# Chunk 0 without the work on its zero state, and four zero fills on GpSimd

## The chip, the cores and the metric

The kernel runs on one core of a Trainium2 chip. The metric is the device time of one execution in microseconds. Three runs of the kernel before took 1280.0, 1281.79 and 1282.41 us, median 1281.79; the execution that the profiler recorded took 1282.63 us, and its trace spans 1280.9 us from the first to the last instruction.

## The reference

Three layers follow each other. The first is a recurrence over 768 steps for 4 x 8 heads with a 40 x 40 state that begins as zero:

```python
state = zeros(B, H, 40, 40)
for t in range(768):
    y[t]  = einsum('bhd,bhde->bhe', r[t], state)
    Sa    = einsum('bhde,bhe->bhd', state, a[t])
    state = state * w[t][:, :, None, :] - outer(Sa, b[t]) + outer(v[t], k[t])
```

Its output, 3072 rows of 320, goes through two gated layers: `(silu(x @ w_gate) * (x @ w_val)) @ w_out`, and the same with a sigmoid alone as the gate, both 320 to 1536 to 320. All of it is to hold in float32.

## The kernel before

The 768 steps are cut into 12 chunks of 64 (`NCH = 12`, `C = 64`). Inside a chunk the recurrence becomes matrix work: the inputs are scaled by running products of w, a triangular matrix is inverted, and the state passes from one chunk to the next through a few products. Four coroutines carry a chunk m:

- `prep_a(m)` turns the scaled inputs (`an`, `tkb`) on TensorE, copies them out on ScalarE, multiplies them (`kps`, L484), writes `bn` (ScalarE, L493 and L494) and the masked product `lq` (VectorE, L496). For chunks 0 to 3 the scaling comes from scans on VectorE (`first`, `scanned`), for the later ones from `powers`, which works mostly on GpSimd (L237), stores its results to DRAM (L267) and then loads the weights of the next four chunks into the same buffers (L235) and clamps them on VectorE (L240).
- `prep_b(m)` inverts the triangular matrix, `halves` for chunks 0 to 2 and `whole` for the others, mainly in small VectorE steps.
- `cp(m)` is `chain(m)` and then `post(m)`. `chain` copies the state `sT` into `qv` (ScalarE, L678), turns it with `tr4` (L680; the matmuls have the line of the helper, L369) and copies the turned state into `sd` (L681), multiplies (`qps` L688, `ups` L706, `sps` L719), and adds to the state (VectorE, L729 and L730). `post` forms the output: products with the new values (`aps`, L857) masked on VectorE, and then `yps` (L888) as a sum of two parts in one PSUM tile: part 0 is r times the state `sd`, part 1 the rest.
- `ahead(m)` runs a part of the first gated layer on the chunk before.

Beside them `early` and `more` load the gated layer's weights in pieces: a DMA (L996), an absolute value on ScalarE (L1004), a clamp on GpSimd (L1007), four VectorE steps (L1010 to L1016), a cast on ScalarE (L1026) and subtractions and sums on GpSimd (L1028 to L1034).

`first()` prepares chunk 0 in a PSUM region of its own. Its last readers are the copy of the scaling (L212) and that of `pend` (L177) on ScalarE; the banks of that region then serve everything else, `tr4` first.

The order of the program is written by `merge`, which takes steps of the coroutines by weights such as `QB` and `QN`. A planner then sets the order on each engine's queue from it and from a model of how long each instruction takes; each queue is worked in order on the chip, an instruction that waits holds up what stands behind it. The DMAs of the start are issued from one queue (SP).

`static` makes the buffers that stay. One with value 0.0 is put on the list `fills`, and `fill()` writes zeros to all on the list by ScalarE copies of a zero column (L81). It is called for `lq0` alone at L275 and for the rest at L944, in the program's order behind `prep_a(0)`. `ut`, `rbd` and the three `lq` have 2048 elements in each partition, the other buffers 256 to 1280. The values' and r's DMAs write into `ut` and `rbd` (L362, L363).

Of the kernel before, what the change touches and what calls it, by code (L numbers as in the profile page):

```python
# [18 lines left out]
P = 128  # L19
B, H, D = 4, 8, 40  # L20
W = 16
C = 64
# [4 lines left out]
PW = 64 + D  # L27
# [15 lines left out]
def attention(ctx, tc, st, ident, ins, banks, extra, early, more):  # L43
# [4 lines left out]
    nc = tc.nc  # L48
# [3 lines left out]
    dr = ctx.enter_context(tc.tile_pool(name="at_dram", bufs=2, space=DRAM))  # L52


    room, fills = {}, []

    def static(shape, name, val=None, part=None):
        sz = 1
        for x in shape[1:]:
            sz *= x  # L60
        if part is None:
            t = st.tile(shape, F32, tag=name, name=name)
        else:
            if part not in room:
                room[part] = [st.tile([P, 16 * P], F32, tag=part, name=part), 0]
            t, at = room[part]
            room[part][1] += sz
            t = t[:, at : at + sz]
            if len(shape) == 3:
                t = t.rearrange("p (x y) -> p x y", y=shape[2])  # L70
            if len(shape) == 4:
                t = t.rearrange("p (x y z) -> p x y z", y=shape[2], z=shape[3])
        if val == 0.0:
            fills.append(t)
        elif val is not None:
            nc.gpsimd.memset(t, val)
        return t
# [12 lines left out]
    E40 = (slice(0, 40), slice(64, 104))  # L90
# [127 lines left out]
    inv, done, out = {}, set(), {}  # L218
# [68 lines left out]
        )  # L287
    qv = static([P, 2, NS, D], "qv", 0.0, "part3")

    ut = static([P, 8, 4, 64], "ut", 0.0)  # L290
    rbd = static([P, 8, 2, 2, C], "rbd", 0.0)

    sT = static([P, 8, PW], "sT", 0.0, "part2")

# [26 lines left out]
    fills.append(x16)  # L321
    lq += [static([P, NS, 2, C], f"lq{i}") for i in (1, 2)]
    xinv = [static([P, NS, C], f"xinv{i}", part="part1") for i in range(2)]
    fills.extend(lq[1:])

    def loads(m):
        dma = nc.sync.dma_start
# [340 lines left out]
    def chain(m):  # L668
# [5 lines left out]
        def half(hb):  # L674
            pool, tag = ((pqu, "qu"), (pzy, "zy"))[hb]
            sg, s4 = slice(8 * hb, 8 * hb + 8), slice(4 * hb, 4 * hb + 4)
            for h2 in range(2):
                nc.scalar.copy(out=two(Q[E40[h2], h2, sg]), in_=pairs(sT, s4)[E40[h2]])  # L678

            ps = tr4(lambda n: sT[:, 4 * hb + n])  # L680
            nc.scalar.copy(  # L681
                out=sd[0:PW, s4], in_=ps[0:PW].rearrange("p n (h e) -> p n h e", h=2)[..., 0:D]
            )
            qps = pool.tile([P, 8, D], F32, tag=tag, name="qps")
            for n in range(8):
                q = 8 * hb + n
                for h2 in range(2):
                    nc.tensor.matmul(  # L688
                        qps[HALF[h2], n, :],
                        lhsT=L[:, q, h2, :],  # L690
                        rhs=Q[:, h2, q, :],
                        start=True,
                        stop=True,
                        tile_position=(0, 64 * h2),
                    )

            for h2 in range(2):
                nc.gpsimd.memset(L[HALF[1 - h2], sg, h2, :], 0.0)
            yield
            qs = wk.tile([P, 8, D], F32, tag="qs", name="qs", bufs=2)  # L700
            nc.scalar.copy(out=qs, in_=qps)
            ups = pool.tile([P, 8, D], F32, tag=tag, name="ups")
            for n in range(8):
                q = 8 * hb + n
                for h2 in range(2):
                    nc.tensor.matmul(  # L706
                        ups[HALF[h2], n, :], lhsT=X[HALF[h2], q, :], rhs=qs[HALF[h2], n, :], start=True, stop=True
                    )
            for h2 in range(2):
                nc.scalar.copy(out=Q[HALF[h2], h2, sg], in_=ups[HALF[h2]])  # L710
            last = nc.scalar.copy(out=pairs(us[hb]), in_=two(ups))
            if m == 1:
                marks["late"] = last
            yield
            sps = pool.tile([P, 8, D], F32, tag=tag, name="sps")
            for n in range(8):
                q = 8 * hb + n
                for h2 in range(2):
                    nc.tensor.matmul(  # L719
                        sps[E40[h2], n, :],  # L720
                        lhsT=T[:, q, 64 * h2 : 64 * h2 + D],
                        rhs=Q[:, h2, q, :],
                        start=True,
                        stop=True,
                        tile_position=(0, 64 * h2),
                    )
            sh = pairs(sT, s4)
            for e in E40:
                nc.vector.tensor_tensor(out=sh[e], in0=two(sps[e]), in1=sh[e], op=ALU.add)  # L729
            nc.vector.tensor_tensor(  # L730
                out=sh[0:PW],
                in0=sh[0:PW],
                in1=pend[0:PW, s4, :, None].to_broadcast([PW, 4, 2, D]),
                op=ALU.mult,
            )
            yield
# [104 lines left out]
    def post(m):  # L841
        pn = load_p(m)
        done.add(("q", m))
        T, sd = tkb[m % 3], sds[m % 2]
        ys = []
        for bp in range(2):
            ps = tr4(lambda n: us[bp][:, n])
            nc.scalar.copy(
                out=ut[0:PW, 4 * bp : 4 * bp + 4, 0:4:3], in_=ps[0:PW].rearrange("p n (h t) -> p n h t", h=2)
            )  # L850
            am, masked = [None, None], []
            for g2 in range(2):
                aps = pzy.tile([P, 2, 2, 2 * C], F32, tag="zy", name="aps")
                for n in range(2):
                    for h2 in range(2):
                        x = 4 * bp + 2 * g2 + n
                        nc.tensor.matmul(  # L857
                            aps[:, n, h2],
                            lhsT=ut[0:PW, x, 2 * h2 : 2 * h2 + 2].rearrange("p u s -> p (u s)"),
                            rhs=rbd[0:PW, x, h2].rearrange("p b t -> p (b t)"),  # L860
                            start=True,
                            stop=True,
                        )
                am[g2] = wk.tile([P, 2, 2, 2, C], F32, tag="am", name="am", bufs=2)
                masked.append(
                    nc.vector.tensor_tensor(  # L866
                        out=am[g2].rearrange("p n h b t -> p (n h b) t"),
                        in0=aps.rearrange("p n h (b t) -> p (n h b) t", b=2),
                        in1=mask[:, None, :].to_broadcast([P, 8, C]),
                        op=ALU.mult,  # L870
                    )
                )
                yield
            yps = pzy.tile([P, H, D], F32, tag="zy", name="yps")
            mats = []
            for part in range(2):
                for h in range(H):
                    hp, h2 = divmod(h, 2)
                    for b2 in range(2):
                        if part == 0:  # L880
                            x = 4 * bp + hp
                            lhs, rhs = rbd[0:PW, x, h2, b2], sd[0:PW, x, h2]
                        else:
                            q = 8 * bp + 2 * hp + b2
                            lhs, rhs = am[hp // 2][:, hp % 2, h2, b2], T[:, q, 64 * h2 : 64 * h2 + D]
                        with group(m, not mats):
                            mats.append(
                                nc.tensor.matmul(  # L888
                                    yps[HALF[b2], h, :],
                                    lhsT=lhs,  # L890
                                    rhs=rhs,
                                    start=part == 0 and h == 0,
                                    stop=part == 1 and h == H - 1,
                                    tile_position=(0, 64 * b2),
                                )
                            )
            if m >= FEW:
                tied(mats, masked)
            ysb = wk.tile([P, DM + 64], F32, tag="ysb", name="ysb", bufs=3)
            yf, pf = yps.rearrange("p h d -> p (h d)"), pn[:, DM * bp : DM * bp + DM]  # L900
            freed[:] = [
                nc.vector.tensor_tensor(out=ysb[:, x:y], in0=yf[:, z : z + y - x], in1=pf[:, z : z + y - x], op=ALU.mult)  # L902
                for x, y, z in ((0, DM, 0), (DM, DM + 64, 256))
            ]
            ys.append(ysb)
            yield
        out[m] = ys
# [32 lines left out]
    QW = (0.12, 0.2)  # L940
    QP = (0.02, 0.2)
    QN = (0.0714, -3)
    merge([(prep_a(0), 1, 0)])
    fill()  # L944
    for t, step in ((x16, 17), (xs, 34)):
        t = t.rearrange("p r t -> p (r t)")[:, ::step]
        nc.gpsimd.tensor_copy(out=t, in_=odd[:, 0:1].to_broadcast([P, 16]) if step == 34 else less.to_broadcast([P, 16]))
# [605 lines left out]
```

## Time and profile before

| | us |
|---|---|
| median of the runs | 1281.79 |
| profiled execution | 1282.63 |
| its span | 1280.9 |
| TensorE busy | 1195.3 |
| VectorE busy | 689.2 |
| ScalarE busy | 593.5 |
| GpSimd busy | 554.6 |

The busy times are sums over the whole span; they say which engine has most to do, not which one is waited for at a given time. For that the profile has a chain of waits, followed back from the last instruction, and a table that cuts the span into stretches. The recurrence ends near 640 us; from then on the gated layers run alone. PE is TensorE, PEld its weight load, DVE is VectorE, ACT ScalarE, POOL GpSimd, SP the engine that issues DMAs.

### The profile page before, as it was taken

What the parts mean: (1) busy time and instruction counts of PE and PEld (TensorE: products, weight loads), DVE (VectorE), ACT (ScalarE), POOL (GpSimd) and SP (SyncE); (2) the same over time, 40 slices, a digit from 0 to 9 for tenths busy, and PEclk for the clock granted to TensorE, in tenths of its full rate; (3) what the DMA queues carried; (4) which work ended last, traced back from release to release, by engine and by line L of the source; (5) the groups of instructions that cost most, each with busy time, mean ns of one, the idle gap of its engine ahead of it and who ended that gap; (6) DMA issues with size and microseconds to landing.
All of it is one profiled execution on the core that took longest, in us unless ns stands there. A gap on an engine that the chain in (4) does not pass through costs nothing.

```text
span 1280.9 us, 31386 instructions
## 1 busy us (share of the span) xinstructions
PE 1195.3 (93%) x12545; PEld 1080.0 (84%) x12545; DVE 689.2 (54%) x1432; ACT 593.5 (46%) x1447; POOL 554.6 (43%) x749
## 2 busy tenths in 40 slices
PE   5577989999999999899999999999999999999997
PEld 4467878889899889888898888889888888888886
DVE  6858559866886678875868544456221212121111
ACT  8454655656565655564443434345232323232222
POOL 5667243322332224356865766766322322232222
PEclk8667777999999999989999999999999999999999
DMA  8445544446544655254374543333010101000001
GB/s 220 129 119 144 166 112 126 109 103 156 128 104 115 136 131 118 65 127 129 88 269 128 181 139 135 103 115 91 1 46 1 46 1 34 1 21 1 21 1 25
DMA packets 180460, 124.38 MB, mean 97 GB/s; under 512 B 134608, under 2 KB 160208, under 8 KB 179536
## 3 DMA queue, kind: packets, MB, share of 16 engines
q1 hardware_dynamic: 180144, 122.11, 35.3%
q8 instruction: 101, 1.65, 0.5%
q14 instruction: 55, 0.45, 0.1%
q10 hardware_dynamic: 160, 0.16, 0.1%
HBM read 90.81 MB, written 31.43 MB: 95 GB/s over the span
## 4 chain that ended last, share of the span: by engine, by line
PE 61%; DVE 20%; ACT 8%; DMA 5%; issue 3%; POOL 2%; SPq 1%; DVEq 0%; ACTq 0%; POOLq 0%
PE g L1163 30%; PE po L1124 16%; PE gv L1108 5%; DVE pr L524 4%; DVE part L530 3%; PE kps L484 3%; DMA wt<-in_a_w_dram 2%; PE aps L857 2%; PE tp L369 1%; PE ups L783 1%; DVE lq L496 1%; DVE am L866 1%; ACT bn L494 1%; DVE g L1113 1%; ACT bn L493 1%
## 5 line engine op out<-in xcount | busy, mean ns | idle before, releaser
L1163 PE MATMUL g<-x,w 128*128 128x512 f32 (+1 forms) x1792 | 419.9, 385 | 0.8 <-DVE g L1170 0.7
L1163 PEld LDWEIGHTS g<-x,w 128*128 128x128 f32 x1792 | 323.2, 188 | 61.5 <-PE g L1163 1.1
L1172 POOL TENSOR_TENSOR hl<-g,hh 128x256 fp32r<-128x256 f32 x216 | 161.7, 754 | 282.4 <-ACT hh L1171 254.0
L1170 DVE TENSOR_TENSOR g<-g,g 128x256 f32<-128x256 f32 x216 | 82.1, 419 | 342.8 <-PE g L1163 340.4
L1124 PE MATMUL po<-w,hh 128*128 128x320 f32 x1152 | 233.7, 311 | 0.5 <-ACT hh L1114 0.4
L1124 PEld LDWEIGHTS po<-w,hh 128*128 128x128 f32 x1152 | 187.1, 188 | 9.6 <-ACT hh L1114 0.8
L1108 PE MATMUL gv<-x,w 128*128 128x256 f32 x1152 | 168.3, 293 | 4.8 <-DVE g L1113 2.5
L1171 ACT CAST hh<-g 128x256 fp32r<-128x256 f32 x216 | 86.9, 406 | 178.4 <-PE po L1124 168.3
L1108 PEld LDWEIGHTS gv<-x,w 128*128 128x128 f32 x1152 | 150.1, 195 | 7.7 <-DVE g L1113 3.4
L1124 PE MATMUL po<-w,hl 128*128 128x320 f32 x576 | 151.2, 313 | 3.7 <-POOL hl L1115 3.6
L1167 ACT ACTIVATE g<-g 128x256 f32<-128x256 f32 x216 | 72.9, 381 | 149.7 <-PE g L1163 143.2
L1115 POOL TENSOR_TENSOR hl<-g,hh 128x256 fp32r<-128x256 f32 x72 | 62.2, 864 | 138.8 <-ACT hh L1114 136.0
L1028 POOL TENSOR_TENSOR dt<-dt,w 128x384 f32<-128x384 f32 (+1 forms) x72 | 79.5, 1105 | 90.2 <-ACT w L1026 53.1
L1124 PEld LDWEIGHTS po<-w,hl 128*128 128x128 f32 x576 | 99.6, 188 | 5.4 <-POOL hl L1115 5.0
L496 DVE TENSOR_TENSOR lq<-kps,part 64x256 f32<-64x256 f32 x96 | 40.5, 422 | 78.6 <-ACT bn L494 72.4
L524 DVE TENSOR_TENSOR pr<-part,sn 128x4 f32<-128x4 f32 (+4 forms) x135 | 75.3, 558 | 3.7
L484 PE MATMUL kps<-lq,kbt 104*128 104x128 f32 x384 | 65.3, 323 | 11.5 <-DVE lq L496 8.6
L484 PEld LDWEIGHTS kps<-lq,kbt 104*128 104x128 f32 x384 | 57.0, 227 | 16.1 <-issue 4.5
L1010 DVE TENSOR_SCALAR dt<-dt 128x384 int32<-128x384 int32 (+1 forms) x72 | 40.5, 563 | 53.6 <-POOL dt L1007 53.3
L530 DVE TENSOR_REDUCE part<-pr 128x2 f32<-128x4 f32 (+4 forms) x135 | 66.6, 493 | 2.9
L857 PE MATMUL aps<-rbd,ut 104*128 104x128 f32 x384 | 56.9, 294 | 4.3 <-DVE ysb L902 1.7
L493 ACT ACTIVATE bn<-kps 32x256 f32<-32x256 f32 x96 | 35.8, 373 | 53.1 <-PE kps L484 40.8
(185 smaller groups left out, 1718.9 us busy)
## 6 DMA issues: line engine op xcount, KB each, us to landing
raw<-in_w_dram SPq DMA_DIRECT2D x48, 384.0 KB
xd<-x SPq DMA_DIRECT2D x12, 896.0 KB
x<-xd SPq DMA_DIRECT2D x11, 896.0 KB
raw<-in_w_dram SPq DMA_DIRECT2D x24, 320.0 KB
ld<-in_a_kb_dram SPq DMA_DIRECT2D x22, 320.0 KB
ld<-rd SPq DMA_DIRECT2D x64, 80.0 KB
pn<-pd SPq DMA_DIRECT2D x32, 160.0 KB
ld<-in_a_a_dram SPq DMA_DIRECT2D x12, 320.0 KB
```

The lines of the kernel that those rows point to most:

```text
L484: nc.tensor.matmul(kps[:, n].rearrange("p h t -> p (h t)"), lhsT=kbt[0:PW, n, :], rhs=lq[m % 3][0:PW, 4 * g4 + n].rearrange("p h t -> p (h ...
L524: nc.vector.tensor_tensor(out=o, in0=xs[:, 0:kk, None, 0:n].to_broadcast([P, kk, 2, n]), in1=sn[:, None, n : n + 2, 0:n].to_broadcast([P, ...
L530: nc.vector.tensor_reduce(out=xs[:, 0:kk, n : n + 2], in_=o, axis=AX.X, op=ALU.add)
L857: nc.tensor.matmul(aps[:, n, h2], lhsT=ut[0:PW, x, 2 * h2 : 2 * h2 + 2].rearrange("p u s -> p (u s)"), rhs=rbd[0:PW, x, h2].rearrange("p b ...
L1028: sub(out=tf, in0=tf, in1=w.bitcast(F32), op=ALU.subtract)
L1108: nc.tensor.matmul(gv[n], lhsT=p, rhs=q, start=e == 0, stop=e == len(seq) - 1)
L1124: self.nc.tensor.matmul(ops[u], lhsT=p[:, us], rhs=q, start=first and n == 0, stop=last and n == 2)
L1163: nc.tensor.matmul(gv[k][:, 0:n], lhsT=p, rhs=cols(at), start=e == 0, stop=e == len(seq) - 1)
L1167: nc.scalar.activation(out=g[j], in_=gv[0][:, j], func=AF.Silu if silu else AF.Sigmoid)
L1170: nc.vector.tensor_tensor(out=g[j], in0=gv[1][:, j], in1=g[j], op=ALU.mult)
L1171: nc.scalar.copy(out=hh, in_=g[j])
L1172: self.heng.tensor_tensor(out=hl, in0=g[j], in1=hh.bitcast(F32), op=ALU.subtract)
```

## The change

Three things are edited. In chunk 0 `half` no longer copies the state into `qv`, turns it and copies it into `sd`: the state is zero there, and `qv` holds zeros already. In `post` of chunk 0 only part 1 of `yps` is summed. And `ut`, `rbd`, `lq1` and `lq2` go on a list of their own, `sets`, which GpSimd fills by four memsets; both lists are filled ahead of `prep_a(0)` in the program's order.

```diff
-    room, fills = {}, []
-    def static(shape, name, val=None, part=None):
+    room, fills, sets = {}, [], []
+    def static(shape, name, val=None, part=None, fill=fills):
...
         if val == 0.0:
-            fills.append(t)
+            fill.append(t)
...
-    ut = static([P, 8, 4, 64], "ut", 0.0)
-    rbd = static([P, 8, 2, 2, C], "rbd", 0.0)
+    ut = static([P, 8, 4, 64], "ut", 0.0, fill=sets)
+    rbd = static([P, 8, 2, 2, C], "rbd", 0.0, fill=sets)
...
-    fills.extend(lq[1:])
+    sets.extend(lq[1:])
...
-            for h2 in range(2):
-                nc.scalar.copy(out=two(Q[E40[h2], h2, sg]), in_=pairs(sT, s4)[E40[h2]])
-            ps = tr4(lambda n: sT[:, 4 * hb + n])
-            nc.scalar.copy(
-                out=sd[0:PW, s4], in_=ps[0:PW].rearrange("p n (h e) -> p n h e", h=2)[..., 0:D]
-            )
+            if m:
+                (the same lines)
...
-            for part in range(2):
+            for part in (0, 1) if m else (1,):
...
-                                    start=part == 0 and h == 0,
+                                    start=part == (m == 0) and h == 0,
...
+    fill()
+    for t in sets:
+        nc.gpsimd.memset(t, 0.0)
     merge([(prep_a(0), 1, 0)])
-    fill()
```

## Rows read from the trace of the kernel before

**Rows 1.** The page's chain that ended last, shares of the span by engine.
```profile
PE 61%; DVE 20%; ACT 8%; DMA 5%; issue 3%; POOL 2%; SPq 1%; DVEq 0%; ACTq 0%; POOLq 0%
```

**Rows 2.** Stretches: us, busy us (x instructions) of PE, PEld, DVE, ACT, POOL, clock, DMA.
```profile
100.00:110.00 10.00, 6.04 (x85) 5.38 (x84) 10.00 (x18) 2.63 (x7) 6.74 (x9) 0.57 0.29 81
...
342.00:384.00 42.00, 40.83 (x679) 38.23 (x677) 31.82 (x65) 26.01 (x64) 12.96 (x15) 1.00 0.54 125
...
700.00:800.00 100.00, 100.00 (x523) 87.98 (x522) 52.67 (x113) 41.10 (x105) 67.41 (x91) 1.00 0.44 148
```

**Rows 3.** Order of time, ScalarE, 5 to 26 us: start, us, instruction [idle before <-releaser].
```profile
5.08 1.89 ACT L81 COPY ut<-part 128x2048 f32<-128x2048 f32 x1
...
6.88 1.89 ACT L81 COPY rbd<-part 128x2048 f32<-128x2048 f32 x1
8.68 3.52 ACT L81 COPY part<-part 128x832 f32<-128x832 f32 x6
...
12.41 3.69 ACT L81 COPY lq<-part 128x2048 f32<-128x2048 f32 x2
...
16.10 1.87 ACT L678 COPY part<-part 40x320 f32<-40x320 f32 x4
...
18.59 0.18 ACT L177 COPY pend<-f 104x16 f32<-104x16 f32 x1
...
24.98 0.51 ACT L1026 CAST w<-dt 128x384 fp32r<-128x384 f32 x1 [2.01 <-DVE dt L1011]
```

**Rows 4.** Order of time, TensorE, the product for `pend` and the first turns.
```profile
13.27 0.36 PE L175 MATMUL f<-part 128*104 128x16 f32 x2
...
18.82 1.95 PE L369 MATMUL tp<-ident,part 128*104 128x128 f32 x8 [5.20 <-ACT pend L177]
```

**Rows 5.** The chain of waits, 14 to 85 us: start, us, what.
```profile
14.83 1.50 DVE tkb L208 x2
...
16.49 1.69 DVE wp L240
...
18.25 2.17 POOL wp L237
...
79.36 5.62 DMA wq<-in_a_w_dram
```

**Rows 6.** Order of time, TensorE and VectorE, 78 to 104 us.
```profile
78.13 1.10 PE L369 MATMUL tp<-ident,part 128*104 128x128 f32 x4
...
83.59 1.45 PE L719 MATMUL sps<-part,tkb 128*40 128x40 f32 x46
...
85.18 1.49 DVE L240 TENSOR_SCALAR wp<-wq 128x2560 f32<-128x2560 f32 x1 [7.36 <-DMA wq<-in_a_w_dram]
...
91.06 0.99 DVE L729 TENSOR_TENSOR part<-sps,part 40x320 f32<-40x320 f32 x2
...
94.35 0.48 DVE L730 TENSOR_TENSOR part<-part,pend 104x320 f32<-104x320 f32 x1
...
101.63 1.94 PE L888 MATMUL yps<-part,rbd 104*64 104x40 f32 x32 [1.23 <-DVE am L866]
```

**Rows 7.** Groups by line, GpSimd: shapes xcount | busy us, mean ns | idle before.
```profile
L773 POOL MEMSET lq<- 64x1024 f32 x18 | 17.1, 953 | 20.1 <-PE qps L762 19.6
...
L698 POOL MEMSET lq<- 64x512 f32 x12 | 6.2, 519 | 0.6
```

**Rows 8.** Order of time, GpSimd, two waits before 40 us.
```profile
12.65 0.21 POOL L947 COPY x<-part 128x16 f32<-128x16 f32 x1 [8.96 <-ACT x L81]
...
38.66 1.01 POOL L1028 TENSOR_TENSOR dt<-dt,w 128x384 f32<-128x384 f32 x1 [2.93 <-DVE ds L1015]
```

**Rows 9.** Order of time, a clamp of 640 on VectorE, and GpSimd beside it.
```profile
10.18 0.50 DVE L155 TENSOR_SCALAR s<-s 128x640 f32<-128x640 f32 x1 [1.31 <-DMA s<-in_a_w_dram]
...
26.04 1.30 POOL L1028 TENSOR_TENSOR dt<-dt,w 128x384 f32<-128x384 f32 x1 [0.36 <-ACT bn L494]
...
26.40 1.29 DVE L155 TENSOR_SCALAR s<-s 128x640 f32<-128x640 f32 x1
```

More of the change, by code (lines that the diff above doesn't have):

```diff
@@ L676, in half @@
             sg, s4 = slice(8 * hb, 8 * hb + 8), slice(4 * hb, 4 * hb + 4)
-            for h2 in range(2):
-                nc.scalar.copy(out=two(Q[E40[h2], h2, sg]), in_=pairs(sT, s4)[E40[h2]])
-            ps = tr4(lambda n: sT[:, 4 * hb + n])
-            nc.scalar.copy(
-                out=sd[0:PW, s4], in_=ps[0:PW].rearrange("p n (h e) -> p n h e", h=2)[..., 0:D]
-            )
+            if m:
+                for h2 in range(2):
+                    nc.scalar.copy(out=two(Q[E40[h2], h2, sg]), in_=pairs(sT, s4)[E40[h2]])
+                ps = tr4(lambda n: sT[:, 4 * hb + n])
+                nc.scalar.copy(
+                    out=sd[0:PW, s4], in_=ps[0:PW].rearrange("p n (h e) -> p n h e", h=2)[..., 0:D]
+                )
             qps = pool.tile([P, 8, D], F32, tag=tag, name="qps")
```

## The prediction

> **What bounds the kernel now.** I read the page's chain by engine first, then the table of stretches, then the chain of waits from 0 to 150 us, and last the instructions of each engine in order of time where that chain passes chunk 0.
>
> The chain that ended last is TensorE's for 61% and VectorE's for 20%; ScalarE has 8% and GpSimd 2% [rows 1]. The reader is to see in the stretches where the rest sits: from 700 us on TensorE is busy 100 of 100 us, and in one chunk of the middle it is busy 40.83 of 42 us [rows 2]. Nothing of the change runs there. All that it touches lies before 105 us, where four engines wait for each other in turn. From 100 to 110 us VectorE is busy 10.00 of 10 us while TensorE has 6.04 [rows 2]. So the question is how much earlier VectorE leaves that stretch. A shift there should carry to the end nearly whole: what follows is bound by the order of work on TensorE and VectorE, and the weights that they then need are loaded when buffers come free, which moves with them.
>
> Two chains lead to that stretch, and they meet at 85 us.
>
> Chain A is chunk 0 itself. ScalarE fills buffers until 16.0 us (two of 2048 elements stand last, 12.41 to 16.0), makes four copies of the zero state (16.10 to 18.0), and only then copies `pend` at 18.59 [rows 3]. TensorE had that product ready at 13.63 (13.27 + 0.36), and its next work, the turns of `an`, sat idle for 5.20 us until `pend` was copied, because the first stage's PSUM banks are handed on only then [rows 4]. From there come the keys, the inverse, and at 78 to 85 us chunk 0's products.
>
> Chain B is the powers of w for chunks 4 to 7. VectorE's clamp (16.49) follows the keys, GpSimd's first product begins at 18.25, and after some 50 us of GpSimd work the results are stored and the next weights loaded into the same buffer (5.62 us from 79.36) [rows 5]. They land at 84.98. VectorE sat idle 7.36 us for them at 85.18, with all that stands behind the clamp in its queue, chunk 0's state sum at 91.06 among it [rows 6].
>
> **The change part by part.**
>
> *Fills.* Four of the 2048-element fills leave ScalarE: 1.89 for `ut`, the same for `rbd`, 3.69 for the two `lq` [rows 3], 7.47 us. On GpSimd the trace has 64x512 in 519 ns and 64x1024 in 953 ns [rows 7]; 434 ns for 512 more elements gives an estimate of 953 + 868 = 1.82 us for 2048, so 7.3 us for four. What hides them: GpSimd waited 8.96 us before its copy at 12.65 [rows 8], that is from 3.69 on. If that cover were gone, the powers at 18.25 would begin later by what overhangs, at most 7.3 us. The values' DMA into `ut` and `rbd` waits for these fills; `ut` was ready at 6.97 and would be by 3.69 + 1.82 = 5.5, and `rbd` at 7.3 instead of 8.8, so the DMA queue is not held longer.
>
> *Copies of the state on ScalarE.* Four at the start, 1.87 us together [rows 3], and one behind each group of turns, which the next item takes along.
>
> *What both do to chain A's beginning.* ScalarE would reach the end of the small fills at 5.08 + (12.41 - 8.68) = 8.8 us. `pend` is then bound by its product at 13.63, so about 13.7 instead of 18.59: 4.9 us. How much arrives is open. The keys that come next are multiplied on VectorE until 16.3 [rows 5], so the second step of chain A gains about that much too; but ScalarE's queue holds a cast of weights at 24.98 that waited 2.01 us for VectorE [rows 3], whose operand goes back over GpSimd to the clamp at 16.49, which does not move. Where that cast stays ahead of chunk 0's scalings, the gain ends there: 0. Where the planner puts the scalings ahead, all 4.9 arrives. It makes its order anew from a kernel whose ScalarE is free earlier, and no row tells which; I take half, 2.4, and keep 0 and 4.9 for the range.
>
> *Turns on TensorE.* Eight, in two groups of 1.10 us [rows 6] (one of the two stands there): 2.2 us out of a stretch in which TensorE runs one thing after the other and chunk 0's state product ends at 85.04 (83.59 + 1.45). It would end at 82.8, and with half of the first term at 80.4. VectorE is idle until 85.18 anyway. What decides is whether the state sums (0.99 for two at 91.06, as much for the next two, 0.48 for each of two scalings behind: 2.9 us) [rows 6] (the first of each pair stands there) run in that idle time or stay behind the clamp. In front: 2.9 us less in a stretch where VectorE is the bound. Behind: 0. I take half, 1.5, with 0 and 2.9 as ends.
>
> *Products of the state with r.* 32 matmuls, 1.94 us from 101.63 [rows 6]. VectorE is full there, so I put them at 0, with 1.9 as the other end.
>
> *Port shared by VectorE and GpSimd.* VectorE's clamp of 640 elements takes 0.50 us at 10.18 and took 1.29 us at 26.40, while GpSimd ran a subtraction from 26.04 to 27.34 [rows 9]: it waited about 0.8 us for GpSimd. The new fills may end only at 3.69 + 7.3 = 11.0, so the last can stand in the way of the clamp at 10.18, on chain B's way in. I take 0, with +0.8 as the bound by this row.
> The Trainium skill ("SBUF — State Buffer", section "Who interferes with whom") says that a VectorE instruction in a two-port mode, a `tensor_scalar` among them, and a GpSimd one exclude each other for a whole instruction. The row at 26.40 agrees; by the rule the wait could be a whole fill, 1.82 us, and the sum 1 us worse than by the row. No row here has a zero fill beside such a clamp.
>
> *Sum.* 2.4 + 1.5 = 3.9 us less. The profiled execution took 1282.63 us, 1.73 more than its span; less 3.9 that is 1278.7. It lies 0.84 above the median of the runs, 1281.79, so I forecast 1277.9, rounded to 1278. Ends: 4.9 + 2.9 + 1.9 = 9.7 less (1272.1), and 0.8 more (1282.6) without a change of order to the bad.
>
> **The rivals.**
>
> *Chain B decides alone* (no change). Nothing removed lies on it; the cast keeps its place on ScalarE and the state sums theirs behind the clamp. For it speaks that the next weights landed within 0.1 us of the state product's end, so whatever chain A saves is slack at once. Against it, that GpSimd itself waited 2.93 us at 38.66 for VectorE [rows 8], and so takes part in chain A's delays. Time: 1281.8, with 1.5 us to either side.
>
> *Everything arrives.* The planner puts chunk 0 ahead on both queues, and GpSimd's wait at 38.66 shrinks too. 4.9 + 2.9 = 7.8 less: 1274.0. Against it: three orders must all fall well.
>
> *GpSimd is held longer* (slower). Chunk 0's earlier inverse puts its small VectorE steps ahead of the weights' steps on VectorE, and GpSimd, which works in order, stands at its weight subtraction with the powers behind it. The place is the wait at 38.66, now 2.93 us [rows 8]. Each microsecond more there moves the store, the load and the clamp at 85.18 by as much. One more such wait is +2.9, two are +5.9; the middle gives 1281.8 + 4.4 = 1286.2. It decides from the point where the added wait is longer than what the state sums save (0 to 2.9). For it: chain B has no slack. Against: less work has to be done before 85 us on every engine but GpSimd, which idled.
>
> *A fill in front of the clamp.* The fill that runs at 10.18 holds VectorE's clamp for its whole length by the rows of smaller ones, 1.82 us [rows 7, 9]; chain B is as late, and chain A's gain stays unused: 1283.6. The Trainium skill's page named above has this as its rule.
>
> **How the numbers follow.** Forecast (2.6 to 6.5 us less, its own range 1275.3 to 1279.2): 0.38. Everything arrives: 0.14. Chain B alone: 0.24. Port: 0.06. GpSimd held: 0.18. A measurement of this kernel tells about 0.2%, 2.6 us, from no change. Faster: 0.38 + 0.14 = 0.52. Within: 0.24 + 0.06 = 0.30. Slower: 0.18. For 8 in 10 the range goes from 1271, one beyond the far end of the gains, to 1287, one beyond the middle of the slow case: a new order on the queues can add or take a little anywhere.
>
> **What would show it.** Right: `pend` copied by 14 us; TensorE's idle time before the turns of `an` gone; no fill of 2048 elements on ScalarE but the first; GpSimd's four at 1.8 us before 11 us; the state sums of chunk 0 before the clamp of the second group; VectorE through its full stretch 3 to 5 us earlier, and the same distance at the first wide matmul of the next stage near 699 us. Wrong: the cast of weights still ahead of the first scaling with the same time at both; the second load into the powers' buffer no earlier than 79.4 and all VectorE work behind it; or a later GpSimd chain, with its waits on VectorE grown. If the distance is there at 110 us and gone at 700, the claim that a shift carries is wrong.

## The result, and the profile after

Four runs of the changed kernel took 1291.32 to 1297.23 us, median 1293.58; four of the kernel before 1280.0 to 1282.41, median 1281.24. The ratio is 1.0102, with a 95% interval from 1.0076 to 1.0128. The change costs 12.3 us; 1278 had been forecast. The profiled execution took 1297.23 us, its span is 1295.5.

The page's chain by engine hardly differs from [rows 1]:

```profile
PE 62%; DVE 19%; ACT 8%; issue 4%; DMA 4%; POOL 3%; SPq 0%; ACTq 0%; POOLq 0%; DVEq 0%
```

The stretches of [rows 2], with the same columns, show that TensorE is as busy in the middle as before (40.74 of 42 us) and nearly so from 700 us on (98.18 of 100). Most of the loss lies between them:

```profile
100.00:110.00 10.00, 7.75 (x55) 7.36 (x52) 9.14 (x23) 3.65 (x8) 7.34 (x8) 0.66 0.61 200
342.00:384.00 42.00, 40.74 (x672) 38.07 (x673) 31.20 (x64) 25.48 (x62) 12.59 (x16) 1.00 0.55 123
700.00:800.00 100.00, 98.18 (x506) 85.21 (x505) 56.18 (x122) 39.61 (x101) 65.17 (x89) 1.00 0.43 140
```

The start of the changed kernel in order of time, engine by engine. A line of the kernel before has 1 more here from L680 on, and 3 more from L947 on (L1113 is now L1116):

```profile
2.38 1.81 POOL L946 MEMSET ut<- 128x2048 f32 x1
4.12 1.81 POOL L946 MEMSET rbd<- 128x2048 f32 x1
5.86 3.55 POOL L946 MEMSET lq<- 128x2048 f32 x2
...
4.64 5.19 DVE L155 TENSOR_SCALAR sn<-sn 128x640 f32<-128x640 f32 x1 [1.54 <-DMA sn<-in_a_w_dram]
...
11.54 2.40 PE L162 MATMUL f<-ident,bn 128*64 128x64 f32 x40 [11.54 <-DVE bn L147]
...
17.95 0.17 ACT L177 COPY pend<-f 104x16 f32<-104x16 f32 x1 [2.42 <-PE f L175]
...
19.88 1.53 PE L369 MATMUL tp<-ident,part 128*104 128x128 f32 x8 [1.97 <-DVE part L169]
```

The fills take 1.8 us each, as estimated. But VectorE's first clamp, for which all of chunk 0 waits, begins at 4.64 and lasts 5.19 us, to 9.83: it ends when the last fill (5.86 + 3.55 = 9.41) is over, and 0.42 us of its own. [Rows 9] have the same clamp of 640 elements at 0.50. So `pend` is copied at 17.95, only 0.64 us earlier than in [rows 3], and the turns of `an` begin 1.06 us later than in [rows 4].

At 82 us chunk 0's state sums (L730 here) have moved ahead of the clamp of the second group, as the prediction wanted; in [rows 6] they stood behind it at 91.06:

```profile
81.85 0.99 DVE L730 TENSOR_TENSOR part<-sps,part 40x320 f32<-40x320 f32 x2 [0.15 <-PE sps L720]
...
86.92 1.49 DVE L240 TENSOR_SCALAR wp<-wq 128x2560 f32<-128x2560 f32 x1 [1.71 <-DMA raw<-in_w_dram]
```

In these two traces the last step of a chunk's inverse (L617 for the first chunks, L534 for the later ones) comes 3.3 us earlier than before at 131 us, 7.1 earlier at 222, 1.7 at 256, at the same time at 301 and 0.8 later at 509. Then the next chunks' `ups` come 4.8 us late (559.1 for 554.3) and 7.5 late (603.2 for 595.7); a `g` of the next layer (L1170 before) is 13.8 us late at 691, and the spans end 14.6 apart. The gain is given back near 260 us, and the loss begins near 540 and grows in steps until about 700.

Only the first of these steps is followed here. VectorE's `g` is the product that a gated layer takes on; ScalarE casts it to `hh` for TensorE, and GpSimd makes `hl` of what the cast leaves over. `am` (L866) is the masked product of `post`; `pr` (L524) and the sum behind it (L530) are steps of the inverse. Before, in order of time:

```profile
538.53 0.41 DVE L1113 TENSOR_TENSOR g<-gv,g 128x256 f32<-128x256 f32 x1
538.87 0.56 DVE L524 TENSOR_TENSOR pr<-part,sn 128x400 f32<-128x400 f32 x1
...
539.44 0.86 PE L1124 MATMUL po<-w,hh 128*128 128x320 f32 x4
...
540.72 1.12 PE L857 MATMUL aps<-rbd,ut 104*128 104x128 f32 x8
542.63 1.13 PE L888 MATMUL yps<-part,rbd 104*64 104x40 f32 x32 [0.79 <-DVE am L866]
543.58 1.11 PE L888 MATMUL yps<-tkb,am 128*64 128x40 f32 x32
...
546.27 0.90 PE L1054 MATMUL xtp<-ident,ysb 128*128 128x128 f32 x3 [1.58 <-DVE ysb L902]
```

and after:

```profile
539.20 0.35 DVE L1018 TENSOR_SCALAR ds<-dt 128x384 int32<-128x384 int32 x1
539.87 0.55 DVE L1019 SCALAR_TENSOR_TENSOR ds<-raw,ds 128x384 f32<-128x384 uint32 x1
540.33 0.57 DVE L524 TENSOR_TENSOR pr<-part,sn 128x400 f32<-128x400 f32 x1
540.93 0.57 DVE L530 TENSOR_REDUCE part<-pr 128x20 f32<-128x400 f32 x1
541.42 0.41 DVE L1116 TENSOR_TENSOR g<-gv,g 128x256 f32<-128x256 f32 x1
...
542.33 1.28 PE L1127 MATMUL po<-w,hh 128*128 128x320 f32 x4 [2.73 <-ACT hh L1117]
...
544.54 2.07 PE L858 MATMUL aps<-rbd,ut 104*128 104x128 f32 x8 [0.41 <-DVE am L867]
547.40 1.94 PE L889 MATMUL yps<-part,rbd 104*64 104x40 f32 x32 [0.78 <-DVE am L867]
549.13 1.91 PE L889 MATMUL yps<-tkb,am 128*64 128x40 f32 x32
...
551.71 0.90 PE L1057 MATMUL xtp<-ident,ysb 128*128 128x128 f32 x3 [0.67 <-DVE ysb L903]
```

`g` is 2.9 us later, and TensorE stands 2.73 us for it. VectorE's queue now has four weight steps ahead of it (L1013 to L1019, two of them shown) and one pair of inverse steps more than before, the two of 400 elements at 540.33 and 540.93. The products that follow take 2.07 for 1.12 us and 1.94 for 1.13. The stretches tell why; the third number from the end is the granted clock. Before:

```profile
540.00:543.00 3.00, 2.19 (x24) 1.67 (x25) 2.96 (x6) 0.43 (x1) 0.27 (x1) 1.00 0.16 55
543.00:551.00 8.00, 6.42 (x127) 5.90 (x123) 7.77 (x12) 3.50 (x9) 3.47 (x5) 0.64 0.70 172
```

After:

```profile
540.00:543.00 3.00, 0.67 (x3) 0.67 (x4) 2.93 (x6) 0.41 (x1) 0.58 (x1) 0.92 0.45 129
543.00:551.00 8.00, 6.81 (x77) 6.00 (x75) 7.22 (x10) 0.85 (x2) 0.16 (x1) 0.50 0.24 75
```

Behind the wait TensorE has the lower of its two clocks all through; before, it had it for a part of that stretch. VectorE is busy 2.96 and 2.93 us of the first 3, so whatever its queue puts ahead of `g` or `am` there makes them later.

### The profile page after: what moved, and what is told of

It is laid out like the page before. It is cut to its first block, busy times and chain, and to the rows that moved or that the text cites. A ratio compares the mean times of both kernels' runs of the same rounds, so it can differ in the third digit from the quotient of the medians.

```text
span 1295.5 us, 31265 instructions
## 1 busy us (share of the span) xinstructions
PE 1197.2 (92%) x12473; PEld 1081.2 (83%) x12473; DVE 688.7 (53%) x1432; ACT 584.2 (45%) x1437; POOL 563.9 (44%) x753
## 4 chain that ended last, share of the span: by engine, by line
PE 62%; DVE 19%; ACT 8%; issue 4%; DMA 4%; POOL 3%; SPq 0%; ACTq 0%; POOLq 0%; DVEq 0%
PE g L1166 30%; PE po L1127 16%; PE gv L1111 4%; DVE pr L524 3%; PE kps L484 3%; DVE part L530 2%; PE aps L858 2%; PE tp L369 2%; DMA wt<-in_a_w_dram 2%; ACT bn L493 1%; ACT bn L494 1%; DVE am L867 1%; DVE dt L1014 1%; PE ups L784 1%; DVE lq L496 1%
## 5 line engine op out<-in xcount | busy, mean ns | idle before, releaser
L1127 PE MATMUL po<-w,hh 128*128 128x320 f32 x1152 | 237.4, 313 | 5.8 <-ACT hh L1117 5.4
L1111 PE MATMUL gv<-x,w 128*128 128x256 f32 x1152 | 171.0, 298 | 8.6 <-DVE g L1116 5.4
L1111 PEld LDWEIGHTS gv<-x,w 128*128 128x128 f32 x1152 | 153.4, 200 | 12.4 <-DVE g L1116 7.6
L1127 PE MATMUL po<-w,hl 128*128 128x320 f32 x576 | 154.5, 315 | 6.3 <-POOL hl L1118 5.6
L1170 ACT ACTIVATE g<-g 128x256 f32<-128x256 f32 x216 | 73.0, 382 | 153.9 <-PE g L1166 145.2
L524 DVE TENSOR_TENSOR pr<-part,sn 128x4 f32<-128x4 f32 (+4 forms) x135 | 74.3, 551 | 3.7
L484 PE MATMUL kps<-lq,kbt 104*128 104x128 f32 x384 | 62.1, 312 | 8.7 <-DVE lq L496 6.6
L530 DVE TENSOR_REDUCE part<-pr 128x2 f32<-128x4 f32 (+4 forms) x135 | 66.6, 493 | 2.9
L858 PEld LDWEIGHTS aps<-rbd,ut 104*128 104x128 f32 x384 | 52.2, 210 | 12.4 <-DVE am L867 8.7
L1007 ACT ACTIVATE dt<-raw 128x384 f32<-128x384 f32 (+1 forms) x72 | 38.4, 534 | 53.3 <-POOL w L1035 38.2
```

What stands on the lines that cost most here:

```text
L484: nc.tensor.matmul(kps[:, n].rearrange("p h t -> p (h t)"), lhsT=kbt[0:PW, n, :], rhs=lq[m % 3][0:PW, 4 * g4 + n].rearrange("p h t -> p (h ...
L524: nc.vector.tensor_tensor(out=o, in0=xs[:, 0:kk, None, 0:n].to_broadcast([P, kk, 2, n]), in1=sn[:, None, n : n + 2, 0:n].to_broadcast([P, ...
L530: nc.vector.tensor_reduce(out=xs[:, 0:kk, n : n + 2], in_=o, axis=AX.X, op=ALU.add)
L858: nc.tensor.matmul(aps[:, n, h2], lhsT=ut[0:PW, x, 2 * h2 : 2 * h2 + 2].rearrange("p u s -> p (u s)"), rhs=rbd[0:PW, x, h2].rearrange("p b ...
L1111: nc.tensor.matmul(gv[n], lhsT=p, rhs=q, start=e == 0, stop=e == len(seq) - 1)
L1127: self.nc.tensor.matmul(ops[u], lhsT=p[:, us], rhs=q, start=first and n == 0, stop=last and n == 2)
```

## The experiments

Two theories. *Order*: the change makes the planner set other queues, and these, not the changed work, cost the late 13 us. *Pace*: the changed work itself shifts the arrival of weights against the recurrence, and the late loss follows from that in any order. Each run was timed in five rounds beside the kernel before, whose medians then were 1279.8 to 1281.7 us; a time stands with its ratio to the kernel before and the 95% interval. Single executions of one kernel lie up to 12 us apart (e13), so verdicts go by the ratios, and distances between two traces serve only to find places.

**Each half alone.** e1 has the fills and the old chunk 0, e2 the new chunk 0 and the old fills; against the changed kernel:

```diff
# e1
-            if m:
+            if True:
...
-            for part in (0, 1) if m else (1,):
+            for part in (0, 1):
...
-                                    start=part == (m == 0) and h == 0,
+                                    start=part == 0 and h == 0,
# e2
-    ut = static([P, 8, 4, 64], "ut", 0.0, fill=sets)
+    ut = static([P, 8, 4, 64], "ut", 0.0, fill=fills)
... (rbd and the two lq in the same way)
+    merge([(prep_a(0), 1, 0)])
     fill()
-    for t in sets:
-        nc.gpsimd.memset(t, 0.0)
-    merge([(prep_a(0), 1, 0)])
```

> The four fills on GpSimd, both lists filled early; chunk 0 keeps the work on its zero state. Order theory (the 13 us come from another order on the queues in the last part of the recurrence, which only both halves of the change together bring about): this kernel's queues are those of the kernel before from about a quarter of the program on, so 1281 +- 4 us. Port theory (the fills hold VectorE's first clamp for 5 us, and that costs the time): 1286 or more.

> Chunk 0 without the work on its zero state; all fills stay on ScalarE where they were. Order theory: queues as before from a fifth of the program on, less work ahead of it, 1277 to 1282 us. Pace theory (the earlier chunk 0 itself, whatever the order, meets a lower clock or other transfers later): 1290 or more.

e1: 1277.80, ratio 0.9978 (0.9962 to 0.9993). e2: 1273.39, 0.9927 (0.9898 to 0.9955). Both halves gain, e2 more than either of its theories had, and e1 although its first clamp too lasts 5.13 us; together they lose 12.3: no sum of local costs does that. In their traces VectorE, ScalarE and GpSimd have the order of before from the first quarter on, but for a few entries; only with both halves do neighbours change again, between some 40 and 80% of the queue (VectorE's to 90%), for up to two thirds of the entries in a tenth of ScalarE's and GpSimd's.

**The late order, taken away and put in.** From here on some kernels have a written order. `QUEUES` lists each engine's instructions in the order of another kernel, and each gets a dependency on the one ahead of it that adds no wait:

```diff
+def pin(tc):
...
+    known = {i.name: i for i in tc.nc.cur_bb.bb.instructions}
+    for names in json.loads(zlib.decompress(base64.b85decode(QUEUES))).values():
+        names = [x for x in names if f"I-{x}" in known]
+        for x, y in zip(names[1:], names):
+            tc.add_manual_dep(known[f"I-{x}"], f"I-{y}", mybir.DependencyInfo(
+                mybir.DependencyClass.NoSync, mybir.DependencyReason.DATA), reason="order on the engine")
...
+    pin(tc)
```

e3 is the changed kernel with the order of before on the last 70% of each queue; e4 is the kernel before with the changed kernel's order there.

> The whole change, with its own order in the first 30% of each engine's instructions and the order of the kernel before forced on the rest. Order theory: the 3 us that the changed kernel was ahead at 255 us stay or are lost, the 13 us are gone: 1277 to 1283 us. Pace theory: 1290 to 1297 us as the changed kernel.

> The kernel before, all its work, with the changed kernel's order forced on the last 70% of each engine's instructions. Order theory: 1290 to 1297 us without any of the change. Pace theory: 1281 us.

e3: 1279.66, 0.9994 (0.9977 to 1.0011). e4: 1293.38, 1.0083 (1.0056 to 1.0109). The loss goes with the order, with the work on either side. The stretches 510 to 600 and 600 to 705 us, before, e3 and e4 in turn:

```profile
510.00:600.00 90.00, 83.07 (x1355) 78.21 (x1352) 60.62 (x127) 47.88 (x114) 45.23 (x64) 0.96 0.41 116
600.00:705.00 105.00, 99.29 (x844) 92.92 (x843) 81.84 (x168) 45.33 (x111) 71.61 (x94) 1.00 0.49 155
```
```profile
510.00:600.00 90.00, 83.41 (x1384) 78.55 (x1384) 60.40 (x127) 47.99 (x115) 45.70 (x64) 0.96 0.43 118
600.00:705.00 105.00, 99.59 (x847) 93.26 (x847) 81.15 (x168) 45.75 (x111) 71.94 (x94) 1.00 0.48 155
```
```profile
510.00:600.00 90.00, 80.88 (x1234) 75.91 (x1235) 58.40 (x122) 44.74 (x105) 42.27 (x56) 0.91 0.39 104
600.00:705.00 105.00, 96.87 (x869) 92.48 (x868) 76.42 (x150) 43.71 (x109) 69.30 (x94) 0.93 0.47 152
```

In the first e4 does 1234 matmuls where the others do 1355 and 1384, at a granted clock of 0.91 for 0.96. The pace theory falls.

**What the parts are worth with the order held.** All queues in the order of before, with chunk 0 alone (e5), the fills alone (e6) and both (e7); the edit is `pin(tc)`.

> Chunk 0 without the products, turns and copies of its zero state, fills as before, and every engine's queue in the order of the kernel before: what the removed work is worth by itself, with no re-planning. The prediction's own sum, with no port and the fills still on ScalarE, was the turns, copies and state sums (-1.5 us) and the products r x state (0 to -1.9 us), carried whole: 1278 to 1280. Queue-order theory: the 7 to 8 us that this half won with its own queues are partly the order's, so here the gain is smaller, 1277 to 1280. Rival (the removed work itself is worth it, order or not): 1273 to 1274, as with its own queues.

> The four fills on GpSimd, chunk 0 as before, every queue in the order of the kernel before. The first clamp on VectorE should again take 5.2 us and the first turns start 4.4 us later. Theory (local effect of the fills is a late start of chunk 0, paid back only in part by the freed ScalarE): 0 to 4 us slower, 1281 to 1285, and the lead of 5 us that the fills alone had with their own queues was the order's. Rival (the freed ScalarE stretch is worth more than the late clamp costs): 1277 to 1279 as with its own queues.

> The whole change with every queue in the order of the kernel before, so that neither the first nor the last part is re-planned. Queue-order theory: no late loss (as with the late order alone put back), and the lead that the change has up to 255 us is no longer lost near 260 us, since there too it was the new order: 1275 to 1279. Rival (the lead near 260 us is lost to a transfer whose time does not depend on the order): 1279 to 1282, no better than with the late order alone put back.

e5: 1279.08, 0.9992 (0.9981 to 1.0004). e6: 1284.16, 1.0035 (1.0022 to 1.0047). e7: 1284.69, 1.0034 (1.0023 to 1.0046). The removed work is worth 0.8 us, no more than the noise; the fills cost 4.3 us alone, and 5.6 on top of the removed work. e7's expectation of 1275 to 1279 failed, and so did its rival: in the order of before the change has no lead that could be lost near 260 us; so the lead that the changed kernel had was its early order's.

**The clamp.** e10 is e7 with the first two fills behind VectorE's first clamp and the other two behind its second:

```diff
...
-        nc.vector.tensor_scalar(out=xw, in0=xw, scalar1=WLOW, scalar2=WHIGH, op0=ALU.max, op1=ALU.min)
+        clamps.append(nc.vector.tensor_scalar(out=xw, in0=xw, scalar1=WLOW, scalar2=WHIGH, op0=ALU.max, op1=ALU.min))
...
-    for t in sets:
-        nc.gpsimd.memset(t, 0.0)
+    held = [nc.gpsimd.memset(t, 0.0) for t in sets]
...
     merge(start)
+    for k, x in enumerate(held):
+        tc.add_manual_dep(x.ins, clamps[k // 2].ins.name, mybir.DependencyInfo(
+            mybir.DependencyClass.Sync, mybir.DependencyReason.DATA), reason="behind a clamp")
```

> The whole change in the queue order of before, with one thing moved: the first two fills on GpSimd wait for VectorE's first clamp, the other two for its second clamp, so that neither stands behind fills. With the fills in front the same kernel was 4.9 us slower than before. Port theory (the held clamp is nearly all of it): the clamp takes 0.5 us again, the first turns start near 7.1 us, and the time is 1278 to 1281. Rival (fills on GpSimd hurt elsewhere, by later holds of VectorE or by what stands behind them in GpSimd's queue): 1283 to 1286, as with the fills in front.

1278.55, 0.9990 (0.9974 to 1.0007): 6.1 us less than e7, as the port theory has it. Its start in order of time:

```profile
4.54 0.49 DVE L155 TENSOR_SCALAR sn<-sn 128x640 f32<-128x640 f32 x1 [1.45 <-DMA sn<-in_a_w_dram]
...
5.16 1.81 POOL L945 MEMSET ut<- 128x2048 f32 x1 [1.47 <-DVE sn L155]
...
9.67 3.55 POOL L945 MEMSET lq<- 128x2048 f32 x2 [0.49 <-DVE s L155]
...
13.22 0.17 ACT L177 COPY pend<-f 104x16 f32<-104x16 f32 x1 [2.15 <-PE f L175]
...
15.42 1.72 PE L369 MATMUL tp<-ident,part 128*104 128x128 f32 x8 [2.23 <-DVE part L169]
```

The clamp is back at 0.49, `pend` is copied by 14 us, as the prediction had it, and the turns begin 3.4 us earlier than in [rows 4]. Yet the end is only 1.2 us earlier, which the interval does not tell from nothing. These four kernels have one order; where their chains stand, in us against the kernel before:

| | turns of `an` (chain A) | GpSimd's first power (chain B) | second group's clamp | end (medians) |
|---|---|---|---|---|
| e5 | -1.92 | -0.42 | -0.17 | -0.8 |
| e6 | +1.06 | +3.40 | +3.13 | +4.3 |
| e7 | +1.05 | +3.39 | +3.39 | +4.8 |
| e10 | -3.40 | -1.07 | -1.74 | -1.2 |

The clamp of the third column is the row at 85.18 in [rows 6]. In e7 and in e10 it waits as long as there for the load that ends chain B:

```profile
88.57 1.49 DVE L240 TENSOR_SCALAR wp<-wq 128x2560 f32<-128x2560 f32 x1 [7.53 <-DMA wq<-in_a_w_dram]
```
```profile
83.44 1.49 DVE L240 TENSOR_SCALAR wp<-wq 128x2560 f32<-128x2560 f32 x1 [7.40 <-DMA wq<-in_a_w_dram]
```

So at 85 us the held clamp costs through chain B: the clamp of the powers at 16.40 comes later on VectorE, at 19.80 in e7, and GpSimd's 50 us of powers move with it. That the end follows chain B is not shown. The sizes of its columns fit the medians better than chain A's, but e10 frees both chains at once, and the first three columns are of single executions: in e6's own trace the 3.13 us have shrunk to 0.79 at 301 us (L534), and in e10's the 1.74 have grown to 6.24. The -0.42 of e5 is scatter: e4 and e8, which start with all the work of before, have the first power at 17.82 and 17.54, for 18.25 in [rows 5].

**The early order by itself.** e9 is the work of before in the queues of e2; e11 is e10's work in them. The edit is again `pin(tc)`.

> All the work of the kernel before, with every queue in the order that the kernel with chunk 0 alone had (it ran 7 us faster; with the queues of before the same work was worth 0.8 us). If the order made those 7 us, they are here too, less about 1 us: 1273 to 1276. If it takes the removed work and the order together (the room that the left-out products and copies give is what the order fills): 1278 to 1282.

> The change with its fills behind the clamps and every queue in the order of the kernel with chunk 0 alone: the fastest order seen with the port kept free. If what the parts showed adds up, the freed ScalarE and no late loss: 1270 to 1274, at or below the 1273.4 of chunk 0 alone. If the fills still cost 3 to 4 us there: 1276 to 1278.

e9: 1279.80, 0.9998 (0.9982 to 1.0014). e11: 1275.58, 0.9958 (0.9941 to 0.9975). So e2's 7 us need both: the order alone gives 0.0, the left-out work alone 0.8. e11 lies between its two ranges; taking the fills off ScalarE adds nothing to e2, which stays the fastest kernel, ahead of the one before and of the changed one.

**Which queue holds the late loss.** e8 has the changed kernel's late order on TensorE alone, e12 on the other four alone; the work is that of before.

> The work of the kernel before; TensorE's queue alone has the order of the changed kernel over its last 70%, all the others keep the order of before. It tells which queue holds the 12 us that all five cost together. If TensorE's own order is at fault: 1288 to 1294. If it is the order on VectorE, ScalarE and GpSimd (the step that makes the expert part's input stands behind weight steps and inverse steps there, and TensorE only waits for it): 1280 to 1284.

> The work of before; VectorE, ScalarE, GpSimd and SyncE have the order of the changed kernel over their last 70%, TensorE keeps that of before. TensorE's order alone cost 10 us, all of it at one place near 647 us, while the five together lost theirs in steps from 540 to 650 us. If the steps are the other four's: 1288 to 1294, with +6 us by 560 us. If TensorE's order carries the loss however the others stand: 1280 to 1284.

e8: 1289.80, 1.0070 (1.0056 to 1.0085). e12: 1294.76, 1.0116 (1.0095 to 1.0138). The other four queues are enough for the whole loss, in steps from 540 us on (0.8 us over the first of its ranges). TensorE's order alone costs too, and e8's time fits the first of its two expectations, but not the reason: nothing is lost up to 640 us, and then, near the end of the recurrence, TensorE has the next layer's products ahead in its queue and stands for their load:

```profile
648.57 3.76 PE L1163 MATMUL g<-x,w 128*128 128x256 f32 x16 [5.25 <-DMA x<-xd]
```

The two don't add up (10.0 and 15.0, all five 12.9 in e4): each of these kernels mixes two orders, so neither says what share of the loss its queues have in the changed kernel.

**Which entry.** e13 puts four of VectorE's weight steps, 1.6 us, behind the `g` of 541.42, e15 puts them behind that chunk's last inverse step; e14 is the control, the changed kernel with its own order written out.

```diff
# VectorE's queue in e13
-... pr dt ysb ysb part0 dt pr ds part0 ds pr part0 g pr part0 ...
+... pr ysb ysb part0 pr part0 pr part0 g dt dt ds ds pr part0 ...
# and in e15
+... pr ysb ysb part0 pr part0 pr part0 g pr part0 ... x1t dt dt ds ds x x ...
```

> The changed kernel in its own order, but for four of VectorE's 1433 instructions: the four weight steps that stand ahead of the expert part's `g` at 541.4 us stand behind it. Together they take 1.6 us there. In the changed kernel TensorE stood 2.7 us for that `g`, and its next 136 or so matmuls ran at half the clock, 2.6 us longer than before. If that is how the first +5 us of the late loss comes about, the wait falls to about 1.2 us, and the clock either stays (4 us back at 551 us) or still falls (1.6 us back); carried to the end 1289.5 to 1292. Rival (the weights of the next expert, now 1.6 us later, are what is late, and the place is only where it shows): 1293 to 1295, nothing back by 560 us.

> The changed kernel with its own order written out by the same means with which the other orders were put into these kernels. If writing an order out costs nothing by itself: 1292 to 1295, like the changed kernel. If it does, it differs by more than 2 us, and all runs with a written order would have to be read against this one.

> As the pinned changed kernel, but the same four weight steps stand behind the last step of that chunk's inverse (`x1t`), past TensorE's whole wait, not just behind the `g`. Put behind the `g` they only moved the wait: TensorE then stood 2.6 us for `am` instead of 2.6 us for `hh`. If what costs is any 1.7 to 2 us of weight steps on VectorE between the two, because VectorE has no idle time there and TensorE falls to half its clock when it waits, then here TensorE's wait falls below 1 us, the clock stays at full speed through 543 to 551 us, and the next chunk's `ups` starts 3 to 5 us earlier than in the pinned changed kernel; at the end 1291 to 1294 (the later steps of the loss stay). Rival (the weights, 8 us later now, are late themselves and hold ScalarE's queue): no gain by 560 us, 1296 to 1300.

e14: 1296.86, 1.0112 (1.0087 to 1.0137), 1.9 us over its range, but with the ratio of the change itself (1.0102): writing an order out costs nothing that shows. e13: 1297.09, 1.0113 (1.0081 to 1.0144): nothing back, and 2.1 us over even the rival's range. The wait for `hh` went from 2.64 us (e14) to 1.80, and the one for `am` rose from 0.76 to 2.57. TensorE of e13 in order of time:

```profile
540.84 1.33 PE L1127 MATMUL po<-w,hh 128*128 128x320 f32 x4 [1.80 <-ACT hh L1117]
...
545.32 2.07 PE L858 MATMUL aps<-rbd,ut 104*128 104x128 f32 x8 [2.57 <-DVE am L867]
```

e15: 1301.54, 1.0161 (1.0147 to 1.0175), slower still and over both of its ranges. Both waits were short there (1.81 and 0.76), but the clock fell all the same:

```profile
543.00:551.00 8.00, 6.54 (x101) 5.77 (x100) 7.36 (x11) 0.00 (x0) 0.00 (x0) 0.50 0.00 0
```

The 0.00 on ScalarE and GpSimd is the new loss. The DMA queue holds a load into the weights' buffer, and that buffer is free only when the late weight steps have read it: the load is issued at 552.24 (539.40 in e14), with the transfers for `ob`, the layer's output, behind it. ScalarE stands for these, and TensorE's next inputs stand behind that copy in its queue. DMA queue, ScalarE and TensorE of e15:

```profile
552.24 0.33 SPq L999 DMA_DIRECT2D raw<-in_w_dram  x1
552.65 0.38 SPq L1767 DMA_DIRECT2D xs<-ob  x1
...
556.31 0.42 ACT L1766 COPY ob<-po 128x320 f32<-128x320 f32 x1 [15.42 <-DMA xs<-ob]
...
557.69 2.24 PE L1111 MATMUL gv<-x,w 128*128 128x256 f32 x7 [4.66 <-ACT x L1063]
```

Neither try gave anything back. The weight steps as a whole stand earlier (of VectorE's 224 in the last 70% of its queue, 161 stand ahead of a `g` that they stood behind before). But they are only about half of this `g`'s delay: from the inverse's 256-element `pr` to `g` VectorE takes 2.25 us before, 4.57 in the changed kernel, 4.56 in e14 and still 3.47 in e13, where only the pair of inverse steps is left ahead of it. No run moved that pair, or the inverse steps that now stand ahead of `am`. Which entries matter stays open.

## Why the prediction was wrong

The step that failed is the planner's new order, which the prediction put at "a little": in the last part of the queues alone it cost 13.1 us. Two more steps failed beside it, the port and the shift that should carry to the end. The 12.3 us, with the order held or let go one piece at a time (distances to the kernel before, so the steps add up to it by themselves; each is uncertain by some 2 to 4 us):

| step | from | us |
|---|---|---|
| chunk 0's left-out work, order of before | e5 | -0.8 |
| fills on GpSimd, order of before | e7 - e5 | +5.6 |
| the new order of the first part | e3 - e7 | -5.6 |
| the new order of the last part | after - e3 | +13.1 |

- *What bounds the kernel.* Right that TensorE is busy nearly throughout from 700 us on. What failed is the end of that part, "a shift there should carry to the end nearly whole". The lead was there at 97 us (chunk 0's first `am` came at 92.37 for 97.09, 4.7 us earlier; 3 to 5 had been foretold) and gone at 301, which the text named as its own refutation. It was the new order's, not the removed work's: in the old order (e7) the step at 301 comes 3.3 us later than before. Why the lead is lost near 260 us is not settled; there TensorE stands longer for GpSimd's `hl` (before, then after), and the granted clock from 250 to 280 us is 0.89 for 0.94.

```profile
268.32 0.58 PE L1124 MATMUL po<-w,hl 128*128 128x320 f32 x2 [2.74 <-POOL hl L1115]
```
```profile
267.38 0.90 PE L1127 MATMUL po<-w,hl 128*128 128x320 f32 x2 [4.63 <-POOL hl L1118]
```

- *The planner's order.* The text gave it one clause, "can add or take a little anywhere". It was -5.6 and +13.1, and the second is more than the far end of all gains (9.7). With the new order of the last part taken away the change is no slower than the kernel before (e3). No rival had this: "GpSimd is held longer" also starts from the order on VectorE, but before 85 us. A new order is not the only way to the wrong sign: with no new order at all the change is 4.8 us slower (e7), by the port.
- *Port.* Taken as 0 with +0.8 as bound. Measured 4.7 on the clamp (5.19 - 0.49), 6.1 at the end (e7 - e10). I had looked at the clamp at 10.18; the one in the way was chunk 0's own, 5 us ahead, and it waited for three fills, not for one. The rival "a fill in front of the clamp" had the mechanism and nearly the size, 1283.6, at a chance of 0.06; with the order held the change takes 1284.7. The page "SBUF — State Buffer" of the Trainium skill (section "Who interferes with whom") says that of a VectorE instruction in a two-port mode and a GpSimd one, the later is blocked for the whole instruction of the other. The trace agrees and goes further, since the clamp got in behind none of the fills until the last was over.
- *Chain A's beginning, turns, state sums.* -2.4 and -1.5 taken. With the order held and the port free the first came true at its place: `pend` at 13.22, turns 3.4 us earlier (e10); the state sums stay behind the clamp in that order. At the end all of it gave 1.2 us, within the noise. The rival "chain B decides alone" (1281.8, at 0.24) fits this: in e10 VectorE still waits 7.40 us for the powers' load. That the state sums did go ahead of the clamp in the changed kernel brought nothing that lasted.
- *Fills.* 1.82 us estimated, 1.81 measured, done by 9.41, before the 11 foretold. The price was right; what they stood in front of was not.
- *GpSimd is held longer.* Not seen: its wait for VectorE at that subtraction is 1.34 us, for 2.93 in [rows 8]. GpSimd's powers came late because they began late, at 21.65 for 18.25.

## What to carry to other kernels

Where a planner sets the queues, a local edit is two changes, the work and the order: time the new work in the old order and the old work in the new one before anything is said about the edit. Of two chains that meet, ask by such runs which one the rest waits for; here freeing the one with the long wait in sight (`pend`, 5.2 us) gave 1.2 us at the end. Work moved to GpSimd was not free beside VectorE here: look for the first VectorE instruction that the deciding chain needs, and count all GpSimd instructions that stand back to back in front of it.

## What the runs showed of the hardware

A VectorE `tensor_scalar` of 128x640 that became ready in the second of four back-to-back GpSimd fills did not get in between them: it ended 0.42 us after the last (9.83 and 9.41). It took 5.12 to 5.22 us in all eight kernels that begin with these fills, and 0.49 or 0.50 in all others. VectorE's reductions at 2.40 and 2.65 ran beside the first fill in 0.33 and 0.45 us, before in 0.34 and 0.45. And a TensorE wait of 2.73 us in a full stretch was followed by 8 us at a granted clock of 0.50, the lower of its levels, in which the 64 products of `yps` took 3.85 us for 2.24 before. The wait alone does not tell when the clock falls: before, the same stretch was granted 0.64 with no TensorE wait over 1.58 us in it, and in e15 0.50 behind one of 1.81.
